# Second products by seven block products: a fused attention and two feed-forward layers on one Trainium2 core

## The chip, the cores and the metric

The kernel runs on one core of one Trainium2 chip. The metric is the device time of one execution in microseconds (us). Three executions of the kernel before took 1291.26, 1291.34 and 1296.3 us; their median is 1291.34. The engines are called by their names in the profile: PE (matmul), DVE (vector), ACT (scalar), POOL (GpSimd), SP (which issues the DMAs).

## What is computed

Attention over 48 heads (4 batches, 12 heads, 448 positions, head size 64), with RMS-normalised q and k, gives x of 1792 tokens x 768 features. Two feed-forward layers follow:

```
a = x @ w_a;  b = x @ w_b            # 768 -> 1536
x = (a * b) @ w_out                  # 1536 -> 768
h = x @ w_in                         # 768 -> 2048
g = h * clip(h + 3, 0, 6) / 6
out = g @ w_out2                     # 2048 -> 768
```

All is float32. A float32 product is made of three matmuls on rounded parts: each operand is split into a high part (an ACT copy that rounds) and a low part (the operand less its high part, a subtraction on DVE or POOL), and PE sums high x high, high x low and low x high in one bank.

## The kernel before, in words

**Two groups.** Tokens stand as columns, 448 per batch. Batches 0 and 1 (the first group) go through both layers by `layer` while the attention of batches 2 and 3 still runs. Batches 2 and 3 (the second group) go through `layer7(0, ...)` and `layer7(1, ...)` (lines 861 to 1036, called in 1070 and 1071). The change is in the second group and in what prepares its x.

**Blocks.** In the second group x is a 2 x 2 matrix of blocks: features 0 to 383 or 384 to 767 by batch 2 or 3. x11 and x12 are the lower features of the two batches, x21 and x22 the upper. A block is three chunks of 128 features. A pair of weight tiles (two times 128 hidden columns, index i) is the 2 x 2 matrix on the left. `quads` (line 910) makes the first ("up") products of one pair by the seven products of Strassen's method in Winograd's form: seven left operands (four blocks as they are, or sums of blocks, line 893) by seven right ones (`sevens`: b11, t1, b22, b21, t2, t3, t4), 9 matmuls each, 63 per pair where eight block products would take 72. The right operands are sums of x's blocks, made once per layer by `x_maker` (line 810): per chunk four differences and seven splits. Banks of PSUM named a, c and d gather the products of a pair; six takes (copies or additions, lines 943 and 946) leave three of the four output blocks in SBUF, the fourth is read from bank a.

**The second ("down") products.** `down(i)` (line 985) multiplies the pair i of weight tiles by the four gated blocks of the pair in the plain way: 12 outputs (six chunks of 128 features by two batches), 6 matmuls each, and every output is then added to `acc` in SBUF (line 1010; the first pair is copied, line 1007). The left side of a pair is four halves of 384 columns, each split by `halve` (line 879: an ACT copy to the high part, a subtraction to the low part). The gated blocks are split by `split_sum` (line 955), four per pair.

**Order of the work.** In the first layer the two up products of a pair (b, then a) are followed by the gate (line 970); `down` of the pair before stands between the up products of the next. In the second layer (line 975: relu6) `down` of a pair stands two pairs later. The last down of a layer runs over the outputs in `XORDER`, and each finished output goes to `finish`: to `x_maker` of the next layer, or to the store (`put`).

**What sets the order of instructions.** A planner (`Plan`) takes every operation with a due time, a cost on each engine that may run it, what it reads and writes, and the buffers it needs. It walks through time with its own cost figures and gives each free engine the ready operation with the earliest due. The order on each engine is fixed then. Buffers of one kind are handed out in the order in which the program asked for them. Operations that may go to DVE or POOL are written `{"V": ..., "G": ...}`; a cost marked True holds the port that the planner lets only one of the two use at a time. `LW7` (line 90) are the leads before a product's due: 34 us for the DMA of a weight tile, 25 for sums of weights, 20 and 18 for the two parts of a half. `R` (line 33) has the due at which each layer's clock starts. SP loads the weight tiles from a scratch copy in DRAM (`kept`), two tiles per pair and product.

**Buffers in the second group.** Halves: 10 slots (`wb`, four of them views of `w`, two each). Split blocks: 6 (`act`). Right operands of the up products: `xx` in place and 9 `xt`. Weight tiles of up products: 4 slots (`wfx`), of down products 3 (`wf`). Blocks in SBUF (`tmpx`): 17, of which 12 are x's own places once x is split. All eight banks.

Of the kernel before, what the change touches and what calls it, by code (L numbers as in the profile page):

```python
# [23 lines left out]
GB = 2  # L24
# [8 lines left out]
R = ((85.0, 1.515), (255.0, 1.267), (411.278, 1.34), (703.581, 1.0), (950.0, 1.0))  # L33
# [56 lines left out]
LW7 = (34.0, 25.0, 20.0, 18.0)  # L90

# [219 lines left out]
def fused_kernel(ctx: ExitStack, tc: tile.TileContext, nat, qt, gs_in, wpk, outT):  # L311
# [52 lines left out]
    for w in K["wst"]:  # L364
# [3 lines left out]
                for w in K["wst"] for h in range(2)]  # L368
    xf_slots = [Slot(xf[:, i // GB, i % GB], [[True]]) for i in range(NX * GB)]
# [440 lines left out]
    def x_maker(src, key, ahead, after=(), holds=None):  # L810
# [4 lines left out]
        def came(mb, due):  # L815
            m, bi = mb
            due -= ahead
# [5 lines left out]

            def own(name, m, bi):
                hi, lo = xx[:, m, bi, 0], xx[:, m, bi, 1]
                out = parts(m, bi, ("xh", "xl"))
                split(due, (hi, lo), src[:, m, bi], [key(m, bi), *hold((m, bi))], out, "VG")
                sevens[name, j] = (lambda: (hi, lo)), out
# [8 lines left out]
            t3 = buf("tmpx")  # L837

            def minus(after_us, out, x, y, reads, writes, after=()):
                add(due + after_us, vg, lambda e: sub(e, out(), x, y), reads=reads, writes=writes, after=after)  # L840

            minus(0.3, lambda: t3.t, x22, x12, [k12, k22], [t3], after)
            minus(0.2, lambda: x12, x12, x11, [k11, *hold(all4[1])], [k12])
            own("t1", j, 1)
            minus(0.4, lambda: x22, x22, x12, [k12, *hold(all4[3])], [k22])
            minus(0.6, lambda: x21, x21, x22, [k22, *hold(all4[2])], [k21])
            for name, x, reads in (("t2", lambda: x22, [k22, *hold(all4[3])]), ("t3", lambda: t3.t, [t3]),
                                   ("t4", lambda: x21, [k21, *hold(all4[2])])):
                w = buf("xt")
                out = [(w, 0), (w, 1)]  # L850
                add(due + 0.8, {"A": 467}, lambda e, w=w, x=x: e.activation(w.t[:, 0], x(), AF.Copy),
                    reads=reads, writes=out[:1], after=after)
                add(due + 1.8, vg, lambda e, w=w, x=x: sub(e, w.t[:, 1], x(), f32(w.t[:, 0])),
# [7 lines left out]
    def layer7(no, ids, clock, late, finish):  # L861
# [26 lines left out]
        def whole(kind, f, due):  # L888
            w = load(kind, f, due - LW7[0], "wf", None)
            return [halve(lambda h=h: w.t[:, h * PH:(h + 1) * PH].bitcast(F32), [(w, h)], due + 0.1 * h, vg)  # L890
                    for h in range(2)]

# [232 lines left out]
```

## Time and profile before

| what | before |
|---|---|
| median of three executions | 1291.34 us |
| profiled execution | 1294.45 us |
| its span, first to last instruction | 1292.7 us |
| busy: PE, DVE, ACT, POOL | 1261.6, 1021.3, 671.0, 230.6 us |
| mean granted TensorE clock, share of full speed | 0.998 |
| matmuls | 6468 |
| DMA moved | 155.33 MB |

The busy time of an engine is the union of its instructions' durations; register, branch and DMA-issuing instructions are not counted. All times of rows are us from the start of the span, unless marked ns. "L932" is line 932 of the kernel. Helpers record their operations under their own line: L389 is every subtraction by `sub`, L404 and L400 the copies by `copy` on DVE and on ACT.

### The profile page before, as it was taken

How to read it: one execution, taken by the hardware profiler on the slowest of the kernel's cores; microseconds unless marked ns; L12 is line 12 of the kernel's file. 1: busy time of each engine (PE TensorE's matmuls, PEld its weight loads, DVE VectorE, ACT ScalarE, POOL GpSimd, SP SyncE). 2: the span in 40 equal slices, each digit the busy share in tenths (PEclk: the TensorE clock that was granted, in tenths of full speed). 3: DMA queues.
4: the chain of work that ended last, by engine and by line, in shares of the span. 5: the costliest groups of instructions: out<-in, count | busy, mean ns of one | idle time of the engine just before them, and what ended most of it. 6: DMA issues, size and time to landing. Idle time of an engine off the chain costs nothing.

```text
span 1292.7 us, 18152 instructions
## 1 busy us (share of the span) xinstructions
PE 1261.6 (98%) x6468; PEld 1060.6 (82%) x6468; DVE 1021.3 (79%) x1853; ACT 671.0 (52%) x1440; POOL 230.6 (18%) x262
## 2 busy tenths in 40 slices
PE   5999999999999999999999999899999999999998
PEld 3668877777988887887878888799999988899997
DVE  8999999997556798787866866977777778787675
ACT  6996767676234575456766654423322335543330
POOL 3231102211001110111101103303321433100010
PEclk9999999999999999999999999999999999999999
DMA  5466676764324356434433421311211201211012
GB/s 199 128 180 236 211 258 209 267 223 123 99 79 129 97 168 236 144 100 156 146 104 123 150 90 60 111 62 62 74 42 57 86 25 62 74 50 37 25 38 86
DMA packets 52363, 155.33 MB, mean 120 GB/s; under 512 B 5936, under 2 KB 18608, under 8 KB 52272
## 3 DMA queue, kind: packets, MB, share of 16 engines
q1 hardware_dynamic: 52272, 154.16, 36.2%
q8 instruction: 51, 0.84, 0.3%
q14 instruction: 40, 0.33, 0.1%
HBM read 121.90 MB, written 32.24 MB: 119 GB/s over the span
## 4 chain that ended last, share of the span: by engine, by line
PE 83%; DVE 10%; DMA 3%; ACT 2%; issue 1%; SPq 0%; POOL 0%; DVEq 0%; ACTq 0%
PE bank L932 17%; PE bank L675 11%; PE bank L676 11%; PE bank L677 11%; PE bank L590 5%; PE bank L999 5%; PE bank L1000 5%; PE bank L1001 5%; PE bank L563 4%; PE bank L525 3%; PE bank L526 3%; DMA wst<-in_w_dram 1%; PE bank L490 1%; DMA rn<-in_nat_dram 1%; DVE xx L389 1%
## 5 line engine op out<-in xcount | busy, mean ns | idle before, releaser
L675 PE MATMUL bank<-xx,w 128*128 128x448 f32 x480 | 182.2, 380 | 0.6 <-DVE act L389 0.3
L677 PE MATMUL bank<-xx,w 128*128 128x448 f32 x480 | 175.5, 366 | 0.0
L676 PE MATMUL bank<-xx,w 128*128 128x448 f32 x480 | 175.5, 366 | 0.0
L1010 DVE TENSOR_TENSOR acc<-bank,acc 128x448 f32<-128x448 f32 x144 | 89.0, 622 | 57.3 <-PE bank L1001 56.9
L932 PE MATMUL bank<-xx,w 128*128 128x448 f32 x567 | 124.8, 367 | 5.8 <-ACT tmp L400 3.0
L675 PE MATMUL bank<-act,w 128*128 128x448 f32 x336 | 128.0, 381 | 1.7 <-DVE acc L781 1.7
L660 ACT ACTIVATE w<-wf 128x768 fp32r<-128x768 f32 x104 | 85.4, 839 | 81.5 <-PE bank L676 61.5
L389 DVE TENSOR_TENSOR w<-wf,w 128x384 fp32r<-128x384 f32 x198 | 111.8, 600 | 16.1 <-ACT w L660 12.1
L677 PE MATMUL bank<-act,w 128*128 128x448 f32 x336 | 122.9, 366 | 0.0
L676 PE MATMUL bank<-act,w 128*128 128x448 f32 x336 | 122.9, 366 | 0.0
L932 PEld LDWEIGHTS bank<-xx,w 128*128 128x128 f32 x567 | 106.0, 188 | 17.0 <-ACT tmp L400 3.7
L781 DVE TENSOR_TENSOR acc<-bank,acc 128x448 f32<-128x448 f32 x120 | 73.9, 620 | 54.2 <-PE bank L677 53.8
L389 POOL TENSOR_TENSOR w<-wf,w 128x384 fp32r<-128x384 f32 x56 | 60.7, 1095 | 287.6 <-ACT w L660 241.9
L535 ACT ACTIVATE p<-bank,nm,rstd 128x448 f32<-128x448 f32 x131 | 94.4, 723 | 31.0 <-PE bank L579 17.8
L531 DVE TENSOR_REDUCE nm<-bank 128x1 f32<-128x448 f32 x168 | 102.3, 616 | 9.8 <-PE bank L526 5.2
L999 PE MATMUL bank<-act,w 128*128 128x448 f32 x276 | 101.6, 368 | 0.0
L1000 PE MATMUL bank<-act,w 128*128 128x448 f32 x276 | 101.2, 366 | 0.0
L1001 PE MATMUL bank<-act,w 128*128 128x448 f32 x276 | 101.0, 366 | 0.0
L400 ACT ACTIVATE pt<-bank 128x512 f32<-128x512 f32 (+1 forms) x126 | 69.0, 549 | 61.2 <-PE bank L563 51.0
L675 PEld LDWEIGHTS bank<-xx,w 128*128 128x128 f32 x480 | 90.3, 188 | 12.2 <-issue 2.1
L677 PEld LDWEIGHTS bank<-xx,w 128*128 128x128 f32 x480 | 90.2, 188 | 7.5
L932 PE MATMUL bank<-xt,w 128*128 128x448 f32 x432 | 95.4, 366 | 0.4 <-ACT tmp L400 0.4
(197 smaller groups left out, 2725.5 us busy)
## 6 DMA issues: line engine op xcount, KB each, us to landing
wst<-in_w_dram SPq DMA_DIRECT2D x68, 768.0 KB, 5.3
kept<-wf SPq DMA_DIRECT2D x68, 384.0 KB, 2.8
wf<-kept SPq DMA_DIRECT2D x64, 384.0 KB, 3.0
wst<-kept SPq DMA_DIRECT2D x40, 384.0 KB, 3.0
rq<-in_qt_dram SPq DMA_DIRECT2D x48, 224.0 KB, 3.0
rn<-in_nat_dram SPq DMA_DIRECT2D x23, 448.0 KB, 3.9
rv<-in_nat_dram SPq DMA_DIRECT2D x24, 224.0 KB, 2.7
out_dram<-acc SPq DMA_DIRECT2D x24, 224.0 KB, 2.0
```

The source lines that it names most:

```text
L389: e.tensor_tensor(out=out, in0=a, in1=b, op=ALU.subtract)
L531: add(at(u + OC[1]), {"V": 531}, lambda e, s=s, nm=nm: e.tensor_reduce(out=nm.t, in_=s.t[:, :S], axis=AX.X, op=ALU.max, negate=True), read ...
L535: add(at(u + OC[3]), {"A": 704}, lambda e, j=j, s=s, nm=nm, p=p: e.activation(p.t, s.t[:, :S], AF.Exp, bias=nm.t, scale=rstd.t[:, qcol[j]: ...
L660: add(due - LEAD + OW[2], {"A": on_act(DM)}, lambda e: e.activation(w.t[:, 0], wf.t.bitcast(F32), AF.Copy), reads=both, writes=[(w, 0, 0), ...
L675: e.matmul(ps, w.t[:, 0, wsl], xh, start=start, stop=False)
L676: e.matmul(ps, w.t[:, 0, wsl], xl, start=False, stop=False)
L677: e.matmul(ps, w.t[:, 1, wsl], xh, start=False, stop=stop)
L932: e.matmul(out, w.t[:, a, chunk(j)], x, start=first and j + n == 0, stop=j + n == HX + 1, skip_group_check=not first)
L999: e.matmul(ps.t[:, :S], w[r].t[:, 0, sl], x[:, 0], start=r == 0, stop=False)
L1000: e.matmul(ps.t[:, :S], w[r].t[:, 0, sl], x[:, 1], start=False, stop=False)
L1001: e.matmul(ps.t[:, :S], w[r].t[:, 1, sl], x[:, 0], start=False, stop=r == 1)
L1010: add(due, {"V": 535}, lambda e, m=m, bi=bi, ps=ps: e.tensor_tensor(out=acc[:, m, bi], in0=ps.t[:, :S], in1=acc[:, m, bi], op=ALU.add), re ...
```

## The change

The down products of the second group are made by the seven block products too, with the weight pair as the left matrix and the four gated blocks as the right one. `down(pairs, ...)` now takes two or three pairs (`SLICE7`: three and three in the first layer; three, three and two in the second). For each of the seven products and each of three chunks it runs the matmuls of all its pairs into one bank, so banks a, c and d exist three times, one per chunk, and a slice's block sums are taken to `acc` once: seven takes per chunk.

`Left` replaces `left_operands` and `whole` for both kinds of product: two tiles, four sums made in place as their inputs are used up (one `ws` buffer instead of four), seven halves. `Right` makes the seven right operands of a gated pair: four differences in place and seven splits, with leads `LX7`. The splits of the gated blocks move from `gate` and `relu6` to `Right`.

The order of a layer is now: the up products of all pairs of a slice, then the down of the slice. The seven products come in the order `WIDE` where two pairs or a whole slice are run together, `TIGHT` for one pair. Weight tiles of both kinds share seven slots (`wfx` with `wf` added).

`x_maker` gives each of x's sums and splits a due by the product that uses it (`base`, `XLEAD`, `XSTEP`), where before all of a chunk had the due of the output that completed it (less 15 us at the second layer); t3 is made in place of x11 and needs no buffer. The clock of the second layer starts at due 943 instead of 950.

The added code (lines removed are in the listing above):

```diff
-R = ((85.0, 1.515), (255.0, 1.267), (411.278, 1.34), (703.581, 1.0), (950.0, 1.0))
+R = ((85.0, 1.515), (255.0, 1.267), (411.278, 1.34), (703.581, 1.0), (943.0, 1.0))
...
+SLICE7 = ((3, 3), (3, 3, 2))
+XLEAD, XSTEP = -14.0, 3.7
+LX7 = (20.0, 19.0, 18.5)
 def piece_order(up, down, n, k):
...
+    K["wfx"] += K["wf"]
...
-    def x_maker(src, key, ahead, after=(), holds=None):
+    def x_maker(src, key, base, after=(), holds=None):
         def came(mb, due):
             def hold(*those):
+            def at(name):
+                return base + XLEAD + XSTEP * ("b11", "t1", "b22", "b21", "t2", "t3", "t4").index(name) + 0.6 * j
             def own(name, m, bi):
+                split(at(name), (hi, lo), src[:, m, bi], [key(m, bi), *hold((m, bi))], out, "VG")
...
+            def minus(name, out, x, y, reads, writes):
+                add(at(name) - 0.5, vg, lambda e: sub(e, out, x, y), reads=reads, writes=writes, after=after)
+            minus("t1", x12, x12, x11, [k11, *hold(all4[1])], [k12])
+            minus("t2", x22, x22, x12, [k12, *hold(all4[3])], [k22])
+            minus("t3", x11, x22, x11, [k22, *hold(all4[0])], [k11])
+            minus("t4", x21, x21, x22, [k22, *hold(all4[2])], [k21])
+            for name, x, reads in (("t2", x22, [k22, *hold(all4[3])]), ("t3", x11, [k11, *hold(all4[0])]),
+                                   ("t4", x21, [k21, *hold(all4[2])])):
+                w = buf("xt", name)
+                add(at(name), {"A": 467}, lambda e, w=w, x=x: e.activation(w.t[:, 0], x, AF.Copy),
+                add(at(name) + 1, vg, lambda e, w=w, x=x: sub(e, w.t[:, 1], x, f32(w.t[:, 0])),
...
+        class Left:
+            def __init__(self, kind, i, first):
+                w = [load(kind, f, first - LW7[0], "wfx", "wst") for f in (2 * i, 2 * i + 1)]
+                one = buf("ws")
+                self.first, self.s = first, (lambda: one.t, [one])
+                self.a11, self.a12, self.a21, self.a22 = (
+                    (lambda w=w[r], h=h: w.t[:, h * PH:(h + 1) * PH].bitcast(F32), [(w[r], h)])
+                    for r, h in (((0, 0), (1, 0), (0, 1), (1, 1)) if kind == dn else ((0, 0), (0, 1), (1, 0), (1, 1))))
+                self.sum(self.s, self.a21, self.a22, ALU.add, 0.0)
+            def sum(self, out, x, y, op, after_us):
+                add(self.first - LW7[1] + after_us, gv, lambda e: e.tensor_tensor(
+                    out=out[0](), in0=x[0](), in1=y[0](), op=op),
+                    reads=[k for k in (*x[1], *y[1]) if k not in out[1]], writes=out[1], after=ends)
+            def __call__(self, name, due):
+                src = {"a11": self.a11, "s1": self.s, "s4": self.s, "a12": self.a12, "s2": self.a11, "s3": self.a21,
+                       "a22": self.a22}[name]
+                w = halve(*src, due, vg)
+                if name == "a11":
+                    self.sum(self.a21, self.a11, self.a21, ALU.subtract, 0.4)
+                    self.sum(self.a11, self.s, self.a11, ALU.subtract, 0.8)
+                if name == "s1":
+                    self.sum(self.s, self.a12, self.a11, ALU.subtract, 2.0)
+                return w
+        STEPS = {"a11": ("b11", "a", True), "s1": ("t1", "c", True), "s4": ("b22", "c", False), "a12": ("b21", "d", True),
+                 "s2": ("t2", "a", False), "s3": ("t3", "a", False), "a22": ("t4", "a", False)}
+        TAKE = {"a11": [((0, 0), "a", True)], "s1": [((1, 1), "c", True)], "a12": [((0, 0), "d", False)],
+                "s2": [((0, 1), "a", True)], "s3": [((1, 1), "a", False)], "s4": [], "a22": []}
+        BOTH = (0, 1), "c", False
+        WIDE, TIGHT = ("a11", "s1", "s4", "a12", "s2", "s3", "a22"), ("a11", "a12", "s2", "s1", "s3", "s4", "a22")
+        def taken(order, k):
+            name = order[k]
+            both = name in ("s2", "s4") and {"s2", "s4"} <= set(order[:k + 1])
+            return TAKE[name] + [BOTH] * both
+        def product(to, ws, xs, cols, first):
+            def go(e):
+                out, n = to.t[:, :S], len(xs)
+                for j, (w, x, c) in enumerate(zip(ws, xs, cols)):
+                    hi, lo = x()
+                    for a, x, k in ((0, hi, 0), (0, lo, 1), (1, hi, 2)):
+                        e.matmul(out, w.t[:, a, chunk(c)], x, start=first and j + k == 0,
+                                 stop=j + k == n + 1, skip_group_check=not first)
+            return go
+        def take(due, out, keys, from_, first):
+            if first:
+                add(due, {"A": 424, "V": 535}, lambda e: copy(e, out(), from_.t[:, :S]), reads=[from_], writes=keys)
+            else:
+                add(due, {"V": 535}, lambda e: e.tensor_tensor(
+                    out=out(), in0=from_.t[:, :S], in1=out(), op=ALU.add), reads=[from_], writes=keys)
         def quads(todo):
+            order = WIDE if len(todo) > 1 else TIGHT
+            turns = [(q, k) for k in range(7) for q in range(len(todo))]
+            left = [Left(*x, dues[q, 0]) for q, x in enumerate(todo)]
+            ps, t, at = [{} for _ in todo], [{} for _ in todo], [{} for _ in todo]
+                right, b, first = STEPS[order[k]]
+                w, due = left[q](order[k], dues[q, k]), dues[q, k]
+                    ps[q][b] = mbank()
+                to, xs = ps[q][b], [now[right, j] for j in range(HX)]
+                add(due, {"PE": 9 * MM}, product(to, [w] * HX, [x for x, _ in xs], range(HX), first), writes=[to],
+                due += 9 * MM * 1e-3
+                for part, b, copied in taken(order, k):
+                    if copied:
+                        t[q][part] = buf("tmpx")
+                    o, at[q][part] = t[q][part], due + 0.6
+                    take(due, lambda o=o: o.t, [o], ps[q][b], copied)
+                out.append({part: (o, lambda o=o: o.t, at[q][part], False) for part, o in t[q].items()})
         def keep(c, ap, due, in_psum):
...
         def gate(c, ap, due, in_psum, b):
+            return b
         def relu6(c, ap, due, in_psum):
...
+            return r
+        class Right:
+            def __init__(self, parts):
+                self.x = [parts[r, bi] for r in range(2) for bi in range(GB)]
+            def __call__(self, name, due):
+                x11, x12, x21, x22 = self.x
+                if name == "t1":
+                    self.minus(x12, x12, x11, due - LX7[0])
+                if name == "t3":
+                    self.minus(x11, x22, x11, due - LX7[0])
+                c = {"b11": x11, "t1": x12, "b22": x22, "b21": x21, "t2": x22, "t3": x11, "t4": x21}[name]
+                a = buf("act")
+                add(due - LX7[1], {"A": 467}, lambda e: e.activation(a.t[:, 0], c.t, AF.Copy), reads=[c], writes=[(a, 0)])
+                add(due - LX7[2], {"V": (535, True), "G": on_pool(S)}, lambda e: sub(e, a.t[:, 1], c.t, f32(a.t[:, 0])),
+                    reads=[c, (a, 0)], writes=[(a, 1)])
+                if name == "b22":
+                    self.minus(x22, x22, x12, due - LX7[2])
+                if name == "b21":
+                    self.minus(x21, x21, x22, due - LX7[2])
+                return a
+            def minus(self, to, x, y, due):
+                add(due, {"V": (535, True), "G": on_pool(S)}, lambda e: sub(e, to.t, x.t, y.t),
+                    reads=[z for z in (x, y) if z is not to], writes=[to])
+        def down(pairs, first, last):
+            size = len(pairs)
+            dues = [[clock(9 * MM * size / HX) for j in range(HX)] for k in range(7)]
+            left = [Left(dn, i, dues[0][0] + 2.0 * q) for q, i in enumerate(pairs)]
+            right = [Right(acts.pop(i)) for i in pairs]
+            ps = {}
+            for k, name in enumerate(WIDE):
+                x, b, start = STEPS[name]
+                ws = [w(name, dues[k][0] + 0.5 * q) for q, w in enumerate(left)]
+                xs = [r(x, dues[k][0] + 0.5 * q) for q, r in enumerate(right)]
+                for j in range(HX):
+                    due = dues[k][j]
+                    if start:
+                        ps[b, j] = mbank()
+                    to = ps[b, j]
+                    add(due, {"PE": 9 * MM * size / HX}, product(
+                        to, ws, [lambda a=a: (a.t[:, 0], a.t[:, 1]) for a in xs], [j] * size, start),
+                        reads=[(o, a) for o in (*ws, *xs) for a in range(2)], writes=[to])
+                    due += 9 * MM * 1e-3 * size / HX
+                    for (r, bi), b2, copied in taken(WIDE, k) + [((1, 0), "a", True)] * (k == 6):
+                        m = j + HX * r
+                        take(due, lambda m=m, bi=bi: acc[:, m, bi], [("acc", m, bi)], ps[b2, j], copied and first)
+                        if last and (not copied or k == 6):
+                            finish((m, bi), due + 0.5)
+        acts, i = {}, 0
+        for size in SLICE7[no]:
+            pairs = range(i, i + size)
+            while i < pairs.stop:
+                todo = [("b", i), ("a", i)] if no == 0 else [("i", i), ("i", i + 1)] if i == 0 else [("i", i)]
+                got = quads(todo) if i == 0 else [x for t in todo for x in quads([t])]
+                if no == 0:
+                    bs = {k: keep(*x) for k, x in got[0].items()}
+                    acts[i] = {k: gate(*x, bs[k]) for k, x in got[1].items()}
+                    i += 1
+                    for x in got:
+                        acts[i] = {k: relu6(*y) for k, y in x.items()}
+                        i += 1
+            down(pairs, pairs.start == 0, i == n)
...
-    first_x = x_maker(xf, lambda m, bi: ("xf", m, bi), 0.0, ends, held)
+    first_x = x_maker(xf, lambda m, bi: ("xf", m, bi), R[3][0], ends, held)
-    layer7(0, BM[3], pace(*R[3]), LF[2], x_maker(acc, lambda m, bi: ("acc", m, bi), 15.0))
+    layer7(0, BM[3], pace(*R[3]), LF[2], x_maker(acc, lambda m, bi: ("acc", m, bi), R[4][0]))
```

## Rows read from the trace of the kernel before

**Rows 1.** The page's totals: busy us of each engine, share of the span, instructions.

```profile
PE 1261.6 (98%) x6468; PEld 1060.6 (82%) x6468; DVE 1021.3 (79%) x1853; ACT 671.0 (52%) x1440; POOL 230.6 (18%) x262
```

**Rows 2.** The page's chain that ended last, shares of the span by engine.

```profile
PE 83%; DVE 10%; DMA 3%; ACT 2%; issue 1%; SPq 0%; POOL 0%; DVEq 0%; ACTq 0%
```

**Rows 3.** Busy time by stage: us, PE, PEld, DVE, ACT, POOL, clock, DMA, GB/s.

```profile
800.00:850.00 50.00, 46.01 (x220) 40.68 (x220) 46.06 (x77) 21.51 (x44) 22.25 (x19) 1.00 0.31 103
850.00:900.00 50.00, 50.00 (x248) 46.28 (x247) 37.83 (x64) 15.92 (x31) 10.97 (x10) 1.00 0.21 64
...
1050.00:1100.00 50.00, 46.17 (x223) 40.82 (x221) 45.09 (x82) 28.48 (x57) 19.33 (x13) 1.00 0.15 48
1100.00:1150.00 50.00, 49.56 (x243) 45.36 (x244) 38.72 (x69) 22.05 (x44) 6.88 (x7) 1.00 0.18 56
1150.00:1200.00 50.00, 50.00 (x247) 45.96 (x246) 38.65 (x69) 18.33 (x37) 4.19 (x4) 1.00 0.15 48
1200.00:1250.00 50.00, 50.00 (x248) 46.29 (x248) 35.18 (x63) 19.63 (x38) 4.92 (x4) 1.00 0.12 40
1250.00:1293.00 43.00, 38.98 (x190) 34.79 (x188) 23.77 (x40) 4.42 (x8) 1.44 (x1) 0.99 0.18 65
```

**Rows 4.** Waits of PE from 790 us on: us in total, times, longest.

```profile
PE bank L932 <- ACT tmp L400: 3.4, 3, 2.1
PE bank L932 <- DVE xx L389: 1.9, 2, 1.7
...
PE bank L932 <- DVE acc L1010: 0.9, 1, 0.9
```

**Rows 5.** The chain in order of time from 780 us: start, us, what.

```profile
995.37 38.30 PE bank L932 x189
...
1289.02 0.62 DVE acc L1010
```

**Rows 6.** PE's timeline in a second product: start, us, what.

```profile
1061.58 0.36 PE L999 MATMUL bank<-act,w 128*128 128x448 f32 x1
...
1063.20 0.36 PE L1001 MATMUL bank<-act,w 128*128 128x448 f32 x1
```

**Rows 7.** Groups from 703 us on: count, busy us, mean ns, idle before.

```profile
L999 PE MATMUL bank<-act,w 128*128 128x448 f32 x276 | 101.6, 368 | 0.0
...
L882 ACT ACTIVATE w<-ws 128x384 fp32r<-128x384 f32 x66 | 34.2, 521 | 51.5 <-PE bank L932 51.2
...
L999 PE MATMUL bank<-act,wb 128*128 128x448 f32 x60 | 22.2, 371 | 0.3 <-DVE acc L1010 0.3
...
L957 ACT ACTIVATE act<-tmp 128x448 fp32r<-128x448 f32 x21 | 12.0, 574 | 6.1 <-DVE tmp L972 6.0
```

**Rows 8.** DVE's timeline at the second entry: start, us, what.

```profile
1073.54 0.60 DVE L389 TENSOR_TENSOR xt<-acc,xt 128x448 fp32r<-128x448 f32 x1
1074.08 0.61 DVE L389 TENSOR_TENSOR xt<-tmp,xt 128x448 fp32r<-128x448 f32 x1
1074.61 0.61 DVE L389 TENSOR_TENSOR xt<-acc,xt 128x448 fp32r<-128x448 f32 x1
...
1078.43 0.54 DVE L389 TENSOR_TENSOR w<-ws,w 128x384 fp32r<-128x384 f32 x1
1078.90 0.54 DVE L902 TENSOR_TENSOR ws<-wst,ws 128x384 f32<-128x384 f32 x1
1079.37 0.60 DVE L946 TENSOR_TENSOR tmp<-bank,tmp 128x448 f32<-128x448 f32 x1
```

**Rows 9.** POOL's timeline at the same place.

```profile
1074.71 5.59 POOL L389 TENSOR_TENSOR w<-ws,w 128x384 fp32r<-128x384 f32 x1 [9.55 <-ACT w L882]
1080.27 1.00 POOL L389 TENSOR_TENSOR w<-wst,w 128x384 fp32r<-128x384 f32 x1
```

**Rows 10.** The line of the up products: duration ns, first and last start.

```profile
L932 PE MATMUL bank<-xx,w x567: 361/365/476, 817.1 to 1242.4; 128*128 128x448 f32 x189
```

More of the change, by code (lines that the diff above doesn't have):

```diff
@@ L816, in came @@
             m, bi = mb
-            due -= ahead
             there.add(mb)
@@ L907, in layer7 @@
-        STEPS = (("a", "b11", True), ("d", "b21", True), ("a", "t2", False), ("c", "t1", True), ("a", "t3", False),
-                 ("c", "b22", False), ("a", "t4", False))
+        class Left:
[21 more added lines that the diff above has]
+                return w
@@ L920, in quads @@
             for q, k in turns:
-                w = halve(*left[q][k], dues[q, k], vg)
-                name, right, first = STEPS[k]
+                right, b, first = STEPS[order[k]]
+                w, due = left[q](order[k], dues[q, k]), dues[q, k]
                 if first:
-                    ps[q][name] = mbank()
-                to, xs = ps[q][name], [now[right, j] for j in range(HX)]
-                def go(e, to=to, w=w, xs=xs, first=first):
-                    out = to.t[:, :S]
-                    for j, (x, _) in enumerate(xs):
-                        hi, lo = x()
-                        for a, x, n in ((0, hi, 0), (0, lo, 1), (1, hi, 2)):
-                            e.matmul(out, w.t[:, a, chunk(j)], x, start=first and j + n == 0,
-                                     stop=j + n == HX + 1, skip_group_check=not first)
@@ L972, in gate @@
             add(due, cost, lambda e: e.tensor_tensor(out=b.t, in0=ap(), in1=b.t, op=ALU.mult), reads=[c], writes=[b])
-            return split_sum(due + 1, b)
+            return b
         def relu6(c, ap, due, in_psum):
@@ L1016, in finished @@
-        def finished(i, got, bs=None):
-            acts.update({(i, *k): relu6(*x) if no else gate(*x, bs[k]) for k, x in got.items()})
-        def kept_b(got):
-            return {k: keep(*x) for k, x in got.items()}
-        if no:
-            for i, got in enumerate(quads([("i", 0), ("i", 1)])):
-                finished(i, got)
-        else:
-            got = quads([("b", 0), ("a", 0)])
-            finished(0, got[1], kept_b(got[0]))
-        for i in range(1 + no, n):
-            bs = None if no else kept_b(quads([("b", i)])[0])
-            if no == 0 and i < n - 1:
-                down(i - 1)
-            finished(i, quads([(ups[-1], i)])[0], bs)
-            if no:
-                down(i - 2)
@@ L1035, in layer7 @@
-        for i in range(n - 2, n):
-            down(i)
+            return r
[21 more added lines that the diff above has]
+                    reads=[z for z in (x, y) if z is not to], writes=[to])
```

82 lines of the change are left out of this document (removed).

## The prediction

> **What bounds the kernel now.** I read the totals first, then the chain of waits, then busy time by stage, then the waits of PE, then single stretches. The totals have PE busy for 98% of the span [rows 1], and the chain that ended last is 83% PE and 10% DVE [rows 2]: the time is a count of matmuls plus the places where PE stands. The change lies in 800 to 1293 us only. There the stages show two dips of PE, 46.01 us of 50 (800 to 850) and 46.17 of 50 (1050 to 1100), and 0.44 us lost after 1100; the other stages are full [rows 3]. Those 3.99 + 3.83 + 0.44 = 8.3 us are all the idle time there. What ended it are ACT copies of banks, the preparation of x (xx, L389) and evictions of acc [rows 4]; both dips are the entries into a layer of the second group, and in both DVE is at 90% or more of the stage. In the full stages DVE is at about 76%, ACT under 45%, POOL under 25% [rows 3]. The granted clock is 1.00 throughout (0.99 in the last stage), the level of 2.4 GHz.
>
> A run of 189 matmuls without a stop took 38.30 us, 202.6 ns each [rows 5]; in a second product, eight steps took 1063.20 - 1061.58 = 1.62 us, 202.5 ns each [rows 6]. An up product and a down product cost the same per matmul.
>
> **Part 1, matmuls removed.** A pair of rows costs the second product 12 outputs x 6 = 72 matmuls now; by seven products it is 7 x 3 chunks x 3 = 63. There are 6 pairs in the first layer and 8 in the second: 14 x 9 = 126 fewer. The trace has 276 + 60 = 336 of each of the three matmul lines, 1008 = 14 x 72 [rows 7]. 126 x 0.2026 = **25.5 us** off the path. The up products keep their 1260. This term is certain, since PE is the bound everywhere else.
>
> **Part 2, the work that feeds them.** Per pair, the left side of a down goes from 4 halves to 7 halves and 4 sums; each half is one ACT pass (521 ns [rows 7]) and one subtraction on DVE or POOL. The right side goes from 4 splits to 7 splits and 4 differences. Evictions fall: 12 per pair to 21 per slice of two or three pairs, 168 to 105 in all. DVE's own price is the distance of starts when it runs back to back, 0.47 us for 384 columns and 0.535 for 448 [rows 8], not the 0.62 of a lone one.
>
> To see whether that count can be trusted: a pair of the second layer now is 15 ops of 384, 23 of 448 and 3 copies, 7.05 + 12.3 + 1.6 = 21.0 us, in 135 x 0.2026 = 27.4 us of PE, 77%. From 1100 to 1200 DVE was busy 38.72 + 38.65 = 77.4 of 100 us [rows 3]. The count holds, and the 11 ops that POOL took there gave no visible relief.
>
> After the change, second layer: 8 x 22 = 176 ops of 384 (82.7 us); of 448, x 33, bank sums 24, relu6 32, differences 32, splits 56, evictions added to acc 63 - 12 = 51, together 228 (122.0 us). That is 204.7 us, and with half of the 36 copies on DVE (9.6) **214 us, against 1008 x 0.2026 = 204.2 us of PE**. Bounds: 190 if ACT takes all copies and POOL 29 ops as it did after 1050, 224 if DVE takes all. First layer: 6 x 33 = 198 ops of 384 (93.1), 189 of 448 (101.1), half of 54 copies (14.4): 209 us against 1134 x 0.2026 = 229.7; bounds 180 to 223. So DVE, which had a quarter of the time free, has about none left in the second layer. ACT: 14 x 0.521 + 7 x 0.574 [rows 7] = 11.3 us per pair, and seven passes of relu6 and copies at about the same 0.57, 15 us of 25.5: free enough.
>
> Locally it is tighter. A full down of three pairs is 189 matmuls, 38.3 us. It wants 33 ops of 384 and 33 of 448 and, after the first, 21 additions: 44.4 us of DVE. The six act buffers hold two product steps and the ten half buffers three, so about 15 of these ops (7.5 us) can be done ahead, and at its end it must prepare the next up products.
>
> **Part 3, POOL as the way out.** At 1074.71 one 384-column subtraction on POOL lasted 5.59 us; the next, at 1080.27, took 1.00 [rows 9]. Through those 5.59 us DVE ran SBUF-only tensor_tensor ops back to back, and POOL came free just after DVE had turned, at 1079.37, to sums that read a bank [rows 8]. So POOL adds little when DVE is full, and what is planned on it comes late. I take its relief as zero; the bounds are the 29 ops above and, on the other side, rival D.
>
> The Trainium skill, "SBUF — State Buffer", section "Who interferes with whom", says that a VectorE instruction with two SBUF inputs takes the port pair that GpSimd reads through, whole instruction by whole instruction, and that one with a single SBUF input leaves it alone. By that rule the 75 bank sums and evictions of the second layer (40 us) would leave POOL some 40 ops, 19 us off DVE, and the sum would come out as in rival B; the row at 1074.71 agrees with the blocking half, and no run here shows the other half at that density.
>
> **Part 4, order and dues.** All dues only rank: the first product of the second group has due 703.6 and started at 817.1 [rows 10], so every due is long past when it counts. Entry to the second layer: b11 needs outputs that now come at step 4 of 7 of the last down, t1 those of step 5, b22 of step 6, and only b21 and t4 the last; a step is 5.5 us (27 matmuls). The use goes in that order, 3.7 us apart. The same 33 ops thus start up to 16 us earlier and are due singly. At the entry to the first layer x comes from attention at one time, so only the order helps. Alone this could take each dip from 4 us to 1; with DVE full from the down before, I keep 2 in the first and count the second under the load. Bounds: 0 (gone) to 8 (each as long again) for both. The "d" banks: a, c and d want nine of eight banks at step 4, so the third d waits for the first one's eviction, with some 1.8 us to spare less 0.6 for it: nothing, or up to 1 us in each of five downs where DVE is behind. The DMAs of weights stay 2 per pair, on the same queue; seven slots instead of four hold a down's six. The tail (last eviction 0.62 us at 1289.02 [rows 5], then the store) stays.
>
> What cover goes: before, one pair's down ran between two up products, so gating and splitting had 14 us or more of matmuls over them. Now a down follows its last up product at once. Its first step needs only block 11, ready five steps (9 us) before; t1 has 1.8 + 5.5 us for a chain of eviction, gate, difference, ACT pass and subtraction, 5 x 0.6 with hops about 4 us. Covered unless DVE is over 3 us behind.
>
> **The sum.** Idle of PE afterwards: second layer 214 - 204 = 10; first layer's downs (44.4 - 38.3, half of it made ahead) 3; first entry 2; together 15 us, 8.3 before. Change: -25.5 + 15 - 8.3 = -18.8. The profiled execution, 1294.45 us (span 1292.7), becomes 1275.7; it lies 3.1 above the median, so the median goes from 1291.34 to **1272.5**.
>
> **Rivals.** A, the forecast: idle 8 to 22, 1265.5 to 1279.5.
> B, DVE keeps up: bank-reading ops let POOL in, ACT takes the copies, the entries close; idle 1 to 5, centre 3: 1291.34 - 25.5 - 5.3 = 1260.5. For: 190 us against 204. Against: the 90% dips, which already stall PE.
> C, DVE is the bound of the second layer: all copies on it, nothing to POOL, 224 - 204 = 20, with 5 elsewhere: idle 25, 1282.5. For: evictions have the latest dues, so in a backlog banks come free last.
> D, slower: subtractions planned on POOL are locked out behind DVE's unbroken runs. Each uncovered one delays a product by 5.59 - 1.00 = 4.6 us, and since halves are given out in program order nothing passes it. The gain is gone at 25.5 + 8.3 = 33.8 us of idle, 7.3 such events in 35 down steps; ten give 46 us, 1291.34 + 12 = 1303.5. Against: operands lie two to three steps ahead, which covers one such event at a time, and in the stage of the one of 5.59 us all idle of PE together was 3.83 us.
>
> **How the numbers follow.** A 0.55, B 0.19, C 0.15, D 0.11. About 0.5% (6.5 us) is what can be told from no change. Faster than 1284.9: A, B and two thirds of C, 0.84; within: the rest of C and a little of D, 0.07; slower: the rest of D, 0.09. The range 1258 to 1289 leaves out D's most and the lower edge of B.
>
> **What would show it.** Right: 2142 matmuls instead of 2268 in the second group at 202 to 203 ns; 105 takes into acc; DVE at 90% or more from 1050 on; PE idle of 8 to 22 us after 800, ended by DVE or ACT preparation of halves and acts inside downs; the dip at the second entry smaller. B: PE full through the downs and DVE under 90%. C: idle ended by evictions, or by DVE in most steps. D: POOL ops of 3 us and more followed at once by idle PE. The forecast is wrong in its main term if matmuls drift from 202.6 ns, and in its load if DVE stays under 85%.

## The result and the profile after

The changed kernel takes 1280.59 us (median of 4 runs, 1279.26 to 1282.1), the kernel before beside it 1293.82: ratio 0.9891, 95% interval 0.9848 to 0.9933. It is faster by 13 us (14 by the ratio) where 18.8 were forecast. The time lies in the forecast range of 1258 to 1289, 8 us above its centre and 1 us above the interval of rival A, the forecast itself (1265.5 to 1279.5). The profiled execution took 1282.1 us (span 1280.3), 12.35 less than the one of before. The totals of its page, which answer to [rows 1]:

```profile
PE 1243.5 (97%) x6342; PEld 1043.1 (81%) x6342; DVE 1063.4 (83%) x1916; ACT 720.4 (56%) x1539; POOL 296.4 (23%) x317
```

There are 126 matmuls fewer, as counted; DVE has 42 us more, ACT 49, POOL 66. Busy time by stage, the columns as in [rows 3]:

```profile
800.00:850.00 50.00, 48.71 (x239) 44.83 (x240) 45.02 (x81) 24.56 (x50) 25.15 (x20) 1.00 0.33 111
850.00:900.00 50.00, 50.00 (x249) 46.23 (x248) 38.90 (x65) 18.82 (x38) 16.29 (x15) 1.00 0.13 40
900.00:950.00 50.00, 48.91 (x236) 43.72 (x235) 42.45 (x74) 22.32 (x46) 14.33 (x13) 1.00 0.25 80
950.00:1000.00 50.00, 50.00 (x244) 45.41 (x243) 38.21 (x62) 15.98 (x31) 19.11 (x18) 1.00 0.20 64
1000.00:1050.00 50.00, 46.18 (x218) 41.61 (x217) 45.79 (x73) 23.01 (x46) 18.70 (x15) 0.97 0.15 48
1050.00:1100.00 50.00, 45.27 (x203) 40.32 (x202) 48.71 (x90) 30.60 (x61) 20.16 (x13) 0.90 0.15 48
1100.00:1150.00 50.00, 49.55 (x244) 45.57 (x244) 44.82 (x77) 27.25 (x56) 15.44 (x15) 1.00 0.21 66
1150.00:1200.00 50.00, 45.78 (x221) 40.68 (x220) 44.49 (x70) 25.03 (x49) 19.45 (x16) 1.00 0.09 30
1200.00:1250.00 50.00, 50.00 (x248) 46.33 (x248) 45.61 (x77) 24.40 (x48) 18.28 (x16) 1.00 0.17 56
```

PE's idle is 1.29 + 1.09 + 3.82 + 4.73 + 0.45 + 4.22 = 15.6 us from 800 to 1250, and 0.6 after; it was 8.3. DVE stands at 97, 90, 89 and 91% in the four full stages of the second layer, where it was at 90% in the stage of the second entry and at 70 to 77 after it. And the clock column, 1.00 up to 1250 before, has 0.97 and 0.90. What PE waited for (total, times, longest), against [rows 4]:

```profile
PE bank L948 <- DVE acc L956: 6.5, 4, 2.4
PE bank L948 <- DVE tmpx L411: 4.1, 1, 4.1
PE bank L682 <- DVE act L396: 1.7, 1, 1.7
```

The third line lies at 800, in the work before the second group, whose first product starts at 816.2. In the group itself (L948) PE waited 14.8 us: 13.2 for takes, that is additions of block sums (L956) and copies of banks (L411, L407), 1.6 for splits; none of it is put down to halves. The takes into acc are 81 + 12 + 12 = 105, as forecast:

```profile
L956 DVE TENSOR_TENSOR acc<-bank,acc 128x448 f32<-128x448 f32 x81 | 46.9, 615 | 6.1 <-PE bank L948 5.8
...
L411 DVE COPY acc<-bank 128x448 f32<-128x448 f32 x12 | 7.4, 617 | 3.0 <-PE bank L948 3.0
...
L407 ACT ACTIVATE acc<-bank 128x448 f32<-128x448 f32 x12 | 6.5, 539 | 4.5 <-PE bank L948 4.4
```

**The longest stop.** PE's timeline around 1091 (start, us, what):

```profile
1083.58 1.99 PE L948 MATMUL bank<-xt,wb 128*128 128x448 f32 x9
1085.41 1.98 PE L948 MATMUL bank<-xx,w 128*128 128x448 f32 x9
1091.48 3.73 PE L948 MATMUL bank<-xt,w 128*128 128x448 f32 x9 [4.09 <-DVE tmpx L411]
1095.84 3.73 PE L948 MATMUL bank<-xt,w 128*128 128x448 f32 x9 [0.63 <-ACT tmpx L407]
```

Nine matmuls last 1.98 us before the stop and 3.73 after it. The granted clock in three short stretches shows why (columns as before):

```profile
1024.00:1029.00 5.00, 3.93 (x12) 3.54 (x13) 5.00 (x10) 0.68 (x2) 0.00 (x0) 0.66 0.00 0
1029.00:1040.00 11.00, 11.00 (x56) 10.20 (x55) 9.85 (x18) 5.50 (x11) 3.50 (x3) 1.00 0.44 143
...
1091.00:1100.00 9.00, 7.89 (x20) 6.54 (x21) 7.71 (x16) 3.08 (x7) 3.85 (x4) 0.50 0.00 0
```

From 1091 to 1100 it is 0.50, the level of 1.2 GHz, and from 1024 to 1029 it is 0.66, around another stop. What DVE did in those 4.1 us, and POOL beside it:

```profile
1086.53 1.43 DVE L1004 SCALAR_TENSOR_TENSOR tmp<-tmp,tmpx 128x448 f32<-128x448 f32 x1
1087.88 1.41 DVE L1004 SCALAR_TENSOR_TENSOR xf<-xf,tmp 128x448 f32<-128x448 f32 x1
...
1090.82 0.61 DVE L411 COPY tmpx<-bank 128x448 f32<-128x448 f32 x1
```

```profile
1086.15 1.33 POOL L911 TENSOR_TENSOR wf<-wf 128x384 f32<-128x384 f32 x1 [2.37 <-DVE ws L911]
1087.44 1.37 POOL L396 TENSOR_TENSOR w<-wst,w 128x384 fp32r<-128x384 f32 x1
```

The copy of a bank that PE waits for starts at 1090.82, though its product (the first of the third pair, in the seven products' order) had ended near 1078. Ahead of it stand six relu6 ops (L1004; four are left out here), and the two that run beside POOL's subtractions last 1.43 and 1.41 us instead of 0.61. The stop near 1022, in the last down of the first layer, is of the same kind:

```profile
1016.42 6.36 PE L948 MATMUL bank<-act,w 128*128 128x448 f32 x30
1025.07 2.49 PE L948 MATMUL bank<-act,w 128*128 128x448 f32 x6 [2.29 <-DVE acc L956]
```

```profile
1022.43 1.49 DVE L396 TENSOR_TENSOR w<-wst,w 128x384 fp32r<-128x384 f32 x1
1023.85 0.55 DVE L396 TENSOR_TENSOR wb<-wst,wb 128x384 fp32r<-128x384 f32 x1
1024.32 1.68 DVE L956 TENSOR_TENSOR acc<-bank,acc 128x448 f32<-128x448 f32 x3
```

By the program's order the product at 1025.07 is step 3 of the down (s4 by b22), the second into bank c of the first chunk; it needs that bank's take of step 2, which DVE starts at 1024.32 behind halves of weights (L396), one of them of 1.49 us.

### The profile page after: what moved, and what is told of

Read it like the earlier page. It is cut to its first block, busy times and chain, and to the rows that moved or that the text cites. A ratio compares the mean times of both kernels' runs of the same rounds, so it can differ in the third digit from the quotient of the medians.

```text
span 1280.3 us, 18146 instructions
## 1 busy us (share of the span) xinstructions
PE 1243.5 (97%) x6342; PEld 1043.1 (81%) x6342; DVE 1063.4 (83%) x1916; ACT 720.4 (56%) x1539; POOL 296.4 (23%) x317
## 4 chain that ended last, share of the span: by engine, by line
PE 80%; DVE 12%; DMA 3%; ACT 2%; issue 1%; POOL 0%; SPq 0%; DVEq 0%; ACTq 0%
PE bank L948 24%; PE bank L682 12%; PE bank L684 12%; PE bank L683 12%; PE bank L597 6%; PE bank L570 4%; PE bank L532 3%; PE bank L533 3%; DVE w L396 2%; DVE act L396 1%; PE bank L497 1%; DMA rn<-in_nat_dram 1%; DMA wst<-in_w_dram 1%; PE bank L584 1%; DMA wst<-kept 1%
## 5 line engine op out<-in xcount | busy, mean ns | idle before, releaser
L948 PE MATMUL bank<-act,w 128*128 128x448 f32 x720 | 157.7, 368 | 7.4 <-DVE acc L956 6.5
L948 PEld LDWEIGHTS bank<-act,w 128*128 128x128 f32 x720 | 135.4, 189 | 21.1 <-ACT wb L890 2.7
L396 POOL TENSOR_TENSOR w<-wf,w 128x384 fp32r<-128x384 f32 x65 | 73.5, 1141 | 292.3 <-ACT w L667 251.3
L948 PE MATMUL bank<-xx,w 128*128 128x448 f32 x603 | 131.3, 367 | 1.6 <-DVE tmp L956 0.9
L396 DVE TENSOR_TENSOR w<-wf,w 128x384 fp32r<-128x384 f32 x205 | 119.3, 615 | 15.9 <-ACT w L667 12.0
L682 PE MATMUL bank<-act,w 128*128 128x448 f32 x336 | 127.6, 380 | 1.9 <-DVE act L396 1.7
L948 PEld LDWEIGHTS bank<-xx,w 128*128 128x128 f32 x603 | 113.3, 189 | 12.7 <-DVE tmp L956 1.3
L684 PE MATMUL bank<-act,w 128*128 128x448 f32 x336 | 122.8, 365 | 0.0
L683 PE MATMUL bank<-act,w 128*128 128x448 f32 x336 | 122.7, 365 | 0.0
L788 DVE TENSOR_TENSOR acc<-bank,acc 128x448 f32<-128x448 f32 x120 | 74.4, 622 | 55.6 <-PE bank L684 55.0
L407 ACT ACTIVATE pt<-bank 128x512 f32<-128x512 f32 (+1 forms) x126 | 69.1, 550 | 65.6 <-PE bank L570 55.2
L682 PEld LDWEIGHTS bank<-xx,w 128*128 128x128 f32 x480 | 90.2, 188 | 12.3 <-issue 2.1
L948 PE MATMUL bank<-xt,w 128*128 128x448 f32 x414 | 94.9, 376 | 4.7 <-DVE tmpx L411 4.1
L684 PEld LDWEIGHTS bank<-xx,w 128*128 128x128 f32 x480 | 90.1, 188 | 7.6
L683 PEld LDWEIGHTS bank<-xx,w 128*128 128x128 f32 x480 | 90.4, 188 | 6.2
L597 PE MATMUL bank<-pt,rv 128*64 128x448 f32 (+1 forms) x384 | 93.4, 567 | 0.0
```

The costliest lines, as they stand in the source:

```text
L396: e.tensor_tensor(out=out, in0=a, in1=b, op=ALU.subtract)
L407: A.activation(out, in_, AF.Copy)
L597: e.matmul(pv.t[rows, :S], rv.t[own[i], at_v[i]], pt.t[own[i], cols[i]:cols[i] + S], start=k == 0, stop=k == 3)
L682: e.matmul(ps, w.t[:, 0, wsl], xh, start=start, stop=False)
L683: e.matmul(ps, w.t[:, 0, wsl], xl, start=False, stop=False)
L684: e.matmul(ps, w.t[:, 1, wsl], xh, start=False, stop=stop)
```

## The experiments

Two theories stand in the expectations of e1 to e4. Theory 1: DVE is nearly full, and the takes rank last in its queue, so a bank is given back late; rank them first and the idle goes. Theory 2: POOL and DVE hold each other up over SBUF, so ops last longer than planned, and what POOL takes off DVE comes back as stretched ops. From e5 on the question is the second entry. Theory A: the order in which buffers are handed out holds takes back. Theory B, the load: DVE's backlog there (the last down's additions, relu6, x's sums and weights' halves at once); whatever goes first, something else ends the wait.

Idle is the sum of PE's missing busy time from 800 to 1250 us, from the views by stage; the entry is its part from 1000 to 1150. Ratios are to the kernel before on the same chip, with 95% intervals; the runs come from several chips, so compare ratios rather than medians.

| kernel | median us | ratio | idle | entry |
|---|---|---|---|---|
| before | 1294 to 1297 | 1 | 8.3 | 4.3 |
| the change | 1280.59 | 0.9891 (0.9848 to 0.9933) | 15.6 | 9.0 |
| e1 takes first | 1281.72 | 0.9908 (0.9891 to 0.9924) | 15.2 | 9.9 |
| e2 no POOL | 1283.22 | 0.9909 (0.9892 to 0.9926) | 15.1 | 10.9 |
| e3 relu6 holds the port | 1276.30 | 0.9858 (0.9842 to 0.9874) | 11.7 | 6.8 |
| e4 dues alone, on before | 1300.47 | 1.0041 (1.0024 to 1.0059) | 9.1 | 4.9 |
| e5 takes' own line | 1277.64 | 0.9855 (0.9841 to 0.9870) | 13.0 | 8.8 |
| e6 no differences | 1276.82 | 0.9825 (0.9787 to 0.9863) | 12.6 | 9.1 |
| e7 one pair per slice | 1327.36 | 1.0238 (1.0218 to 1.0259) | | |
| e8 four edits | 1280.84 | 0.9879 (0.9859 to 0.9899) | 14.9 | 10.8 |
| e9 e3 and e5 | 1281.20 | 0.9887 (0.9868 to 0.9905) | 14.6 | 9.7 |
| e10 old dues | 1285.77 | 0.9926 (0.9904 to 0.9947) | 21.2 | 11.9 |
| e11 e5 and e6 | 1271.55 | 0.9820 (0.9798 to 0.9842) | 8.4 | 7.9 |
| e12 e1 and e5 | 1280.24 | 0.9878 (0.9861 to 0.9896) | 13.9 | 11.2 |

**e1, takes first.**

```diff
+TAKE_AHEAD = 30.0
...
-                add(due, {"A": 424, "V": 535}, lambda e: copy(e, out(), from_.t[:, :S]), reads=[from_], writes=keys)
+                add(due - TAKE_AHEAD, {"A": 424, "V": 535}, lambda e: copy(e, out(), from_.t[:, :S]), reads=[from_], writes=keys)
...
-                add(due, {"V": 535}, lambda e: e.tensor_tensor(
+                add(due - TAKE_AHEAD, {"V": 535}, lambda e: e.tensor_tensor(
```

> Theory 1 (PE stands because the takes that free banks stand last in a nearly full DVE queue; the half clock follows the longest of these stops): with all takes of the second group ranked 30 us earlier, PE's waits for takes (12 us by the profile of the changed kernel) fall below 4, the idle of PE after 800 us from 16 us to 6 to 9, the half-clock stretches (13.6 us at half speed, some 5 us lost) vanish, time 1280 to 1268-1273. Theory 2 (the lock between POOL and DVE stretches DVE's ops, whatever their order): waits move to halves and acts, idle stays at 14 to 18, time within 3 us of 1280.

No gain. Its stages from 1000 to 1150:

```profile
1000.00:1050.00 50.00, 50.00 (x245) 45.46 (x244) 45.93 (x73) 24.58 (x49) 26.86 (x21) 1.00 0.15 48
1050.00:1100.00 50.00, 40.56 (x177) 34.23 (x176) 48.79 (x77) 25.36 (x51) 28.29 (x19) 0.92 0.15 48
1100.00:1150.00 50.00, 49.50 (x235) 44.38 (x235) 46.47 (x78) 25.89 (x53) 23.79 (x17) 0.98 0.20 64
```

The stop in the down is gone (50.00 where it was 46.18), and the next stage has 9.44 us idle where it had 4.73. Theory 1 fails in its main point: with the takes ranked first the idle is as large, and part of it is now waits for x's preparation. One stop kept its place, though: PE waited 4.8 us for a copy of a bank (L412 here) up to 1093.7, which no rank moved (e5 looks at it, e12 puts the two edits together).

**e2, no POOL.** In `layer7` every cost with two engines keeps DVE alone (x's own sums may still go to POOL):

```diff
-        vg, gv = {"V": (on_dve(PH), True), "G": on_pool(PH)}, {"G": on_pool(PH), "V": (on_dve(PH), True)}
+        vg = gv = {"V": (on_dve(PH), True)}
...
-                add(due, {"V": (535, True), "G": on_pool(S)}, lambda e: sub(e, to.t, x.t, y.t),
+                add(due, {"V": (535, True)}, lambda e: sub(e, to.t, x.t, y.t),
```

> All subtractions and sums of the second group on DVE, none on POOL (x's splits excepted). Theory 1 (DVE's load is what counts, POOL relieves it): some 100 ops of 0.47 to 0.535 us come back to DVE, 50 us, most of it in the second layer where it has none to spare: 1310 to 1330. Theory 2 (POOL gives nothing, each of its ops stretches a DVE op by as much): no DVE op over 0.7 us, time 1275 to 1285.

The time is that of the change, within the intervals. Four stages of the second layer:

```profile
1050.00:1100.00 50.00, 41.21 (x181) 35.44 (x180) 49.36 (x94) 26.80 (x54) 3.20 (x3) 0.93 0.15 48
1100.00:1150.00 50.00, 49.16 (x243) 45.26 (x243) 45.99 (x91) 30.66 (x61) 0.00 (x0) 1.00 0.19 64
1150.00:1200.00 50.00, 49.52 (x245) 45.53 (x244) 47.05 (x92) 26.08 (x51) 0.00 (x0) 1.00 0.10 32
1200.00:1250.00 50.00, 49.42 (x241) 44.60 (x240) 46.75 (x92) 24.14 (x49) 0.00 (x0) 1.00 0.17 56
```

DVE was busy 49.36 + 45.99 + 47.05 + 46.75 = 189.2 us with 369 ops; the changed kernel had 183.6 with 314, and 60 on POOL. 55 more ops cost DVE 5.6 us, 0.10 us each. One group from 850 to 1000 us, first here, then in the changed kernel, shows where POOL's work went:

```profile
L396 DVE TENSOR_TENSOR w<-wst,w 128x384 fp32r<-128x384 f32 x25 | 13.6, 550 | 1.0 <-ACT w L890 1.0
```

```profile
L396 DVE TENSOR_TENSOR w<-wst,w 128x384 fp32r<-128x384 f32 x15 | 11.0, 744 | 1.4 <-ACT w L890 1.4
```

The same 384-column subtraction takes 0.55 us without POOL and 0.74 with it. Theory 2 holds as to the lock: what POOL takes off DVE it gives back, all but 0.10 us per op, by stretching the rest. But nothing is won by leaving POOL out either.

**e3, relu6 holds the port.**

```diff
-            add(due + 0.5, {"V": 535}, lambda e: e.scalar_tensor_tensor(
+            add(due + 0.5, {"V": (535, not in_psum)}, lambda e: e.scalar_tensor_tensor(
```

> The planner is told that relu6's DVE op with both inputs in SBUF holds the shared port, so it plans no POOL op beside it. Theory 2 (lock): those ops last 0.62 instead of up to 1.4 us, the stop of 4.1 us near 1091 is gone, time 3 to 8 us down. Theory 1 (rank of the takes): the stop stays or moves, time within 3 us of 1280.

By the medians 4.3 us below the change, as theory 2 had it, but the intervals of the two ratios overlap. The longest wait at the second entry is 2.1 us instead of 4.1, and of relu6's ops one still lasts 1.17 us, the others 0.63 at most.

**e4, dues alone.** The kernel before with `at(name)` for x's sums, in the order of its own steps.

```diff
-            due -= ahead
...
+            def at(name):
+                return base - 14.0 + 3.7 * ("b11", "b21", "t2", "t1", "t3", "b22", "t4").index(name) + 0.6 * j
```

> The kernel before with only x's sums due by their use, in the old order of products. If the order alone closes the entries: idle after 800 us from 8.3 to about 3, time 4 to 6 us below before. If the entries are bound by DVE's load (90% busy there) whatever its order: idle 7 to 9, no change within 2 us.

Slower than before by 0.4%. The first entry, and the stage behind the second:

```profile
800.00:850.00 50.00, 46.53 (x212) 42.07 (x213) 40.77 (x73) 22.25 (x45) 23.04 (x18) 0.93 0.33 111
...
1100.00:1150.00 50.00, 47.15 (x219) 43.53 (x219) 37.15 (x65) 23.06 (x46) 6.83 (x6) 0.93 0.12 40
```

The idle is 9.1 us where it was 8.3, and two stages have a clock of 0.93 where it was 1.00; the longest waits, 3.2 and 3.1 us, lie there. In the order of before, dues by use are worth nothing.

**e5, the takes' own line.** Block buffers are handed out in the program's order, so the third pair's first copy had to wait until all eight relu6 buffers of the first two pairs were given out.

```diff
-                        t[q][part] = buf("tmpx")
+                        t[q][part] = buf("tmpx", "take")
```

> Block buffers for the takes are handed out in a line of their own, no longer behind the relu6 buffers that the program asked for earlier. Theory A (the 4.1 us stop near 1091, where a copy of a bank waited 12 us after its product, comes from that line): the stop and the 10.2 us of half clock around it are gone, 1280 to 1272-1275. Theory B (DVE's backlog at the second entry): the stop is as long, a few products earlier or later, and the time stays within 3 us of 1280.

The 4.1 us wait for that copy is gone, the ratio is 0.9855; but two others of 2.1 and 2.6 us came, with half clock after each. Of theory A the stop went, as expected; the time is at the edge of theory B's, within 3 us of 1280.

**e6, no differences.** `Right.minus` does nothing: the four differences per pair are left out, 56 ops or 30 us by the planner's cost. In the trace DVE's total falls by 18 us only, from 1063.4 to 1045.3, and by 2.4 from 1000 to 1100, because half of these ops had run on POOL.

> Left out: the four differences per pair on the right side of the down products (56 ops of 448 columns in all), so the output is not the reference's; matmuls, splits and takes stay. Theory B (load of DVE, 56 x 0.535 = 30 us of it): idle after 800 us from 16 to 5 or less, no long stop, 1280 to 1262-1267. Theory A (buffers and ranks): the stops stay where they were, 1276 to 1280.

The idle is not theory B's, and the time is in theory A's range (1276 to 1280). The stop in the second layer's second down is gone (idle of 1150 to 1250 from 4.2 to 0.9), but there are two waits of 3.9 and 4.0 us, one at the end of the first layer's last down (1045) and one at the second entry (1092).

**e7, one pair per slice.**

```diff
-SLICE7 = ((3, 3), (3, 3, 2))
+SLICE7 = ((1,) * 6, (2, *(1,) * 6))
```

> The same seven products but one pair per slice (two in the first of the second layer), so block sums leave PSUM for every pair: 294 takes into acc instead of 105, matmuls the same 2142. Theory B: 189 more DVE ops of 0.535 us, 101 us of DVE time of which at most a third finds room: 1340 to 1370. If DVE's load were not what limits: 1280 to 1295.

47 us slower than the change, where the load theory said 60 to 90. PE's waits:

```profile
PE bank L948 <- ACT act L1023: 25.0, 11, 8.0
PE bank L948 <- DVE acc L956: 6.5, 7, 1.2
```

25.0 us, in 11 waits of 2.3 on average, are waits for the split of a gated block (L1023), 6.5 for takes. By the program's order a down of one pair follows its up product at once, so the chain of take, relu6, difference and split stands open, while a slice of three has two other pairs over it. So this run does not measure the sum in PSUM by itself.

**e8, four edits.** e3 and e5, copies of banks on ACT alone, takes 6 us earlier.

> Four edits together: relu6's op marked as holding the port (1276 alone), the takes' own line of buffers, copies of banks on ACT only, takes ranked 6 us earlier. Theory A: 1264 to 1270. Theory B: the load on DVE falls only by the copies (some 18 of 0.535 us in the second layer), 1271 to 1276.

Neither expectation: no gain over the change, and none over e3 or e5. The idle at the entries is 10.8 us; its longest wait, 4.6 at the second entry, is again for an addition of a bank to a block sum.

**e9, e3 and e5 together.**

> The two edits that helped alone: relu6's op marked as holding the port (ratio 0.9858 to before) and the takes' own line of buffers (0.9855; the changed kernel 0.9891). If they end different stops, their gains of 3.5 to 4.5 us add: idle after 800 us 8 to 10, ratio 0.981 to 0.983. If both only shift the same backlog at the second entry: idle 11 to 13, ratio 0.984 to 0.987.

The ratio is above both expectations: the gains do not add, nothing of them is left. The copy's wait is gone, but PE stands 4.3 us at the same place (1095) for an addition of a bank.

**e10, old dues.** The changed kernel, with each of x's ops due as before.

```diff
-                return base + XLEAD + XSTEP * ("b11", "t1", ...).index(name) + 0.6 * j
+                return due + {"t1": 0.7, "t2": 0.9, "t3": 0.8, "t4": 1.1}.get(name, 0.0)
```

> The changed kernel with x's sums at the dues of before (those of the output that completes a chunk). If the dues by use are worth what the second entry's order promised: both entries stand longer, idle after 800 us 19 to 23, 4 to 8 us above 1280. If they are worth nothing, as in the kernel before: within 2 us of 1280.

0.35% slower than the change by the ratios, whose intervals overlap; idle and time are those of the first expectation. A stage at each entry:

```profile
800.00:850.00 50.00, 44.65 (x205) 38.87 (x204) 46.03 (x79) 20.80 (x42) 17.36 (x14) 0.97 0.30 103
...
1050.00:1100.00 50.00, 43.06 (x197) 37.80 (x198) 49.83 (x83) 26.98 (x54) 24.72 (x19) 0.97 0.18 56
```

The first entry has 5.35 us idle instead of 1.29, the second 6.94 instead of 4.73. With the new order of products, the dues by use are worth 5.6 us of idle.

**e11, e5 and e6 together.**

> The four differences per pair left out as before (output not the reference's) and the takes' own line of buffers. If load and line are two separate causes: idle after 800 us from 12.6 (differences out) and 13.0 (line) to 6 to 8, no half clock at the second entry, 1266 to 1270. If the load at the entry is one backlog that moves: idle 11 to 13, 1274 to 1278.

The best ratio, 0.9820, hardly below e6's, and between the two expectations. The idle is 8.4 us where e6 has 12.6. Its stages:

```profile
1000.00:1050.00 50.00, 46.00 (x218) 41.79 (x217) 43.10 (x69) 24.89 (x52) 14.40 (x12) 0.97 0.16 48
1050.00:1100.00 50.00, 47.19 (x222) 42.20 (x221) 49.11 (x86) 31.80 (x64) 16.38 (x12) 0.97 0.16 48
...
1150.00:1200.00 50.00, 49.97 (x247) 45.88 (x246) 40.47 (x73) 27.27 (x53) 11.14 (x11) 1.00 0.15 48
```

The downs of the second layer are full (49.97 of 50). 4.00 + 2.81 us stay in the last down of the first layer and the second entry, where x's preparation was left whole, and 1.08 in the stage behind.

**e12, e1 and e5 together.**

> Takes ranked 30 us earlier (no stops in the downs of 950 to 1050, but 9.4 us idle at the second entry) and the takes' own line (no 4 us stop at 1091). If stops are independent: idle after 800 us 7 to 10, 1270 to 1274. If DVE's backlog is conserved: 13 to 16, most of it in 1050 to 1110, 1277 to 1282.

Neither the stop in the down nor the long wait for a copy is there, and yet the idle is 13.9 us, now in waits of 2.3 us at most, above all for halves, copies and x's splits. That is theory B's expectation, the backlog conserved:

```profile
1050.00:1100.00 50.00, 42.03 (x193) 35.04 (x192) 48.84 (x75) 25.91 (x52) 26.64 (x21) 1.00 0.16 48
1100.00:1150.00 50.00, 46.74 (x213) 41.48 (x211) 45.97 (x81) 26.66 (x56) 15.44 (x13) 0.93 0.22 64
```

## Why the prediction came out as it did

**Matmuls removed: right.** 6342 is 6468 - 126, mostly at the same pace (nine in 1.98 us with the tail of the last): 25.5 us. Before as after, some up products run at nine in 2.02 us.

**DVE without room, and the idle it leaves: right in size, in part by luck.** Forecast were 15 us of idle, 10 in the second layer, 3 in the first layer's downs, 2 at the first entry. Measured were 4.73 + 0.45 + 4.22 + 0.6 = 10.0, 1.09 + 3.82 = 4.9 and 1.29. DVE's load came as the count of ops said: 214 us in the second layer were forecast with POOL at no relief, and without POOL (e2) DVE was busy 214.5 us from 1050 on. Luck is in the parts: the 4.73 us hold one wait of 4.1 us that ended with the order of buffers (e5), which the sum did not have.

**The step that failed is the sum: it had no term for the clock.** It read 1.00 throughout before and left it there. In the profiled execution, stops of 2.3 and 4.1 us came with stretches at half clock, where the products from 1025 and from 1091 to 1100 ran at half pace, nine in 3.73 instead of 1.98 us. PE was busy there for 3.4 + 8.1 us, so some 5.7 us were lost. -25.5 + (16.2 - 8.3) + 5.7 = -11.9; the spans differ by 12.4, and the 0.5 between the two was not traced. Of the 8 us by which the median missed the centre, the clock is 5.7 and the idle 1.2 (less that 0.5); another 1.6 come from the step from profile to median, since the profiled execution lay 3.1 us above the median before and 1.5 after. The clock is no trait of one execution: the four runs of the change have a mean of 0.992 to 0.996, the ten of the kernel before beside e1 one of 0.997 to 1.000.

**What ends the idle: wrong.** I named halves and splits; it was takes, the sign that stood under rival C. e1 and e12 show that this is where the backlog is seen, not what makes it: with takes first the idle is about the same, and with their own line of buffers too it ends at x's preparation, halves and copies. The bank that stopped PE in the down was a c bank at step 3, not the third d at step 4.

**POOL at zero relief: right, and measured.** Without POOL the second group takes the same time (e2), and an op that POOL had costs DVE 0.10 us. Rival B's 19 us through the gaps of bank-reading ops didn't come. (One reading was off: in the kernel before POOL was busy for 34% of the stage from 1000 to 1050, not under 25%.) The Trainium skill, "SBUF — State Buffer", section "Who interferes with whom", has a VectorE op with two SBUF inputs and a GpSimd op that reads SBUF block each other. The trace agrees, after as before, now with DVE as the one that waits: relu6 ops with both inputs in SBUF took 1.43 and 1.41 us beside POOL ops of 1.33 and 1.37, and 0.61 without. Rival D, late operands from POOL, did not show: PE waited 0.6 us for POOL in all.

**Order and dues: right at the first entry, wrong at the second.** The stage of the first entry went from 3.99 us of idle to 1.29; with the old dues it has 5.35 (e10). Only 2.3 of the 3.99 us lay behind the group's first product (the prediction took all for the entry; 1.7 are waits of the work before, at 803 and 813), and of the 1.29 none does: the entry closed. The same dues in the order of before lose (e4). The dip at the second entry was to be smaller; it grew, from 3.83 to 4.73 us.

**What stays open.** From 1000 to 1150 there are 7 to 12 us of idle in every order of the change that was tried, against 4.3 in the kernel before. That DVE's load there is the cause is argued, not shown: e6 took only 2.4 us off DVE from 1000 to 1100, and its idle there is 9.1. The last down's additions, x's 33 ops and two pairs of weight sums meet there within some 40 us; how much of the idle is their number and how much the order of buffers was not separated, since x's own preparation was never reduced. Each edit also reorders all engines, and e3 and e5, some 0.3% better alone and nothing together (e9), show that gains of this size can't be put to the edit's own account. e3 (1276.30) and e5 (1277.64) are the fastest complete kernels run; their intervals overlap that of the change.

## What to carry to other kernels

Replacing matmuls by sums is a purchase: count the vector engine's time per unit of saved matmul time, and compare it with what that engine has free in the same stage, not over the span. When it comes near full, ranking one kind of work first only moves the stops. Price a stop of the matmul engine above its length, because the half-speed stretch around it can cost as much again: here 4.1 us of stop, and 4 us lost in the 8.1 that PE then ran at half clock.

## What the runs showed of the hardware

- The clock can fall with a short stop: 0.50 for 10.2 us around the stop of 4.1 us here, and 0.66 from 1024 to 1029 around one of 2.3. Not every stop draws it: the waits of up to 2.1 us in the kernel before [rows 4] left the clock at 1.00 [rows 3], and the stop near 1195 in the changed kernel (longest wait 2.4) has 1.00 in its stage. What decides was not tried.
- POOL beside a nearly full DVE gave it 0.10 us of relief per op (e2): a 384-column subtraction on DVE lasted 0.55 us with POOL left out and 0.74 with it at work.
